# Gate rows of an xLSTM, attention and mixer kernel: laid out by kind, first two chunks built on chip, plan renewed

## The chip, the cores and the metric

One Trainium2 chip, one of its cores. The metric is device time in microseconds (us) of one launch; lower is better. Engines: PE multiplies matrices (its weight loads are PEld), DVE and ACT and POOL work on elements, SP issues transfers (its queue is SPq). "Off chip" below is the device memory that holds the inputs and the output.

## The reference

Three stages on a batch of 2 with 768 tokens. First a matrix-memory recurrence with 8 heads of 40 columns, then a two-of-four mixture of causal attention experts, then a mixer over tokens and channels.

```python
for t in range(S):                                   # 768 tokens, batch 2, 8 heads, D = 40
    m_new = np.maximum(f_gate[:, :, t] + m, i_gate[:, :, t])
    f_stab = np.exp(f_gate[:, :, t] + m - m_new)
    i_stab = np.exp(i_gate[:, :, t] - m_new)
    C = f_stab * C + i_stab * outer(vt, kt);  n = f_stab * n + i_stab * kt
    y[:, :, t] = sigmoid(o_gate[:, :, t]) * (C @ qt) / np.maximum(np.abs(n @ qt), 1.0)
# x = y with the heads side by side (320 columns)
# experts e = 0..3: softmax(causal(x wq_e (x wk_e)^T / 8)) (x wv_e) wo_e, weighted for the best 2 of 4
# u = x + (relu(x^T w_tok1) w_tok2)^T;  out = u + relu(u w_ch1) w_ch2
```

## The kernel before

**Stages.** The recurrence is cut into 6 chunks of 128 tokens per batch, so 12 chunks n = 0 to 11. For a chunk, `m_gates` makes the exponents of decay between its tokens as a product of two thin operands: `lt` (left, 128 columns) and the row tile `RT[n % 2]` (right, 4 heads x 128 tokens); ACT takes the exponential into `e`, POOL clears the part above the diagonal. `m_whole` multiplies keys and queries (both in the chunk's `kv` tile), `m_scores` multiplies that by `e` on DVE, `m_carry` and `m_decay` bring in the state `CB` of earlier chunks (through `mc` and `w`), `m_intra` sums over values and ends with x, which is transposed (`turn`) and split into a high and a low part; `m_update` makes the next state with `vs`. Two chunks of x make a stretch of 256 tokens, for which `p_qk` and `p_v` project (tiles `xt`, `wh`, `wl`); then come attention (`a_scores`, `a_unit`, `a_value`, `a_tail`), the token mixer (`t_hidden`, `t_mix`) and the channel mixer (`c_hidden`, `c_out`, 12 slices of 128 channels).

**Gates.** The decay's exponents need running sums and running maxima of the gates (`gt`), which DVE scans make: for chunk 0 in straight code (L385 to L402), for the others in `gates_rest` in pieces of one, two and two chunks. 128 partitions hold two halves of the heads and both batches, 32 each; in each 32 some rows hold a high part, some a remainder, some constants. The result `msp` stands in partitions by head and is wanted along the free axis in two partitions of the row tile, so `load_m` moves it with two transfers of 4 KB on chip (L381) per chunk. Chunk 0 alone goes another way: `lr0` and `m0` (L396 to L402), a product on DVE that spreads the heads.

**Narrowing.** The mixer's weights come as 64-bit words. `narrow` cuts each piece to 32 bits and splits it: an ACT pass (L523), three DVE passes (L526, L528, L531), for a channel piece an ACT copy (L538) and a subtraction on DVE or POOL (L292). Token weights have 8 pieces, channel weights 24.

**Order.** All instructions are put in order at build time by `Plan`: every part yields steps with an engine (or a choice), a cost, the events it waits for and the tiles it takes. The planner starts, again and again, the step that can begin first; among steps of one engine within 0.004 us the lower number in `RANK` wins. `fillers` puts products of a zero tile (`still`, 128 x 128, bf16) on PE wherever the plan has PE waiting in its first 46 us (`FILL`), which keep its clock up. The times in the plan are the planner's; on the chip only the order and the waits remain, so a filler once written is always run. SP issues transfers in the planned order, with at most 8 under way.

Of the kernel before, what the change touches and what calls it, by code (L numbers as in the profile page):

```python
# [24 lines left out]
L = 128  # L25
# [5 lines left out]
ND = 13  # L31
# [6 lines left out]
SML = 35  # L38
# [36 lines left out]
class Plan:  # L75
# [106 lines left out]
    def run(self):  # L182
        while self.live:
# [8 lines left out]
            for e, cs in cand.items():  # L192
                s0 = min(c[0] for c in cs)
                c = min((c for c in cs if c[0] <= s0 + 0.004), key=lambda c: c[1][0])
                if pick is None or c[0] < pick[1][0]:
                    pick = (e, c)
# [56 lines left out]
def fused_kernel(ctx: ExitStack, tc: tile.TileContext, gates0, gates1, kv, og, wqkv, wo, wt12,  # L253
# [50 lines left out]
    plan = Plan(dict(P=1.1, A=7.3, V=7.7, G=6.5, S=3.6),  # L304
                dict(bank=7, page=NS, rows=ROWS - 4, big=ND - 5, e=EB, w=WB, mc=1, rem=1, x=1, vs=4, xp=3, q=2,
                     am=6, atr=2, tile=2, y=2, tf=2, g=1), [0.0] * DEEP + [3.6, 2.5, 6.2, 7.8], fillers)
# [56 lines left out]
    lt = big([128, 2, S], F32R, "lt")  # L363
# [882 lines left out]
```

## Time and profile before

| | |
|---|---|
| Median of 3 runs (lowest, highest) | 357.08 us (356.17, 357.26) |
| The profiled execution | 357.03 us |
| Its span (first to last instruction) | 355.3 us |
| Busy in the span: PE, PEld | 347.2 us (98%), 303.2 us (85%) |
| Busy in the span: DVE, ACT, POOL | 233.7 us (66%), 167.4 us (47%), 37.1 us (10%) |
| Products of the zero tile | 379 of 3213 on PE |
| Bytes moved | 28.9 MB, 81 GB/s over the span |

The span is what the trace shows, the time also has what lies around it (1.73 us here). A busy share is a mean over stages with different limits: PE's 98% contains the zero products, and it is DVE that is busiest beside it until about 140 us. What ends a wait in one stage is read from that stage.

### The profile page before, as it was taken

The page shows a single profiled execution, that of the slowest core. Times are in us where ns is not written, and L with a number is a line of the kernel's source. Part 1 is how long each engine was busy: PE and PEld are TensorE (multiplying, and loading weights), DVE is VectorE, ACT ScalarE, POOL GpSimd, SP SyncE. Part 2 cuts the span into 40 slices and gives each one's busy share as a digit, 9 for nine tenths or more (in the row PEclk, how much of TensorE's full clock was granted, in tenths as well). Part 3 has the DMA queues.
Part 4 walks back from the last instruction along what each step waited for, and adds up shares of the span by engine and source line. Part 5 has one row for each costly group of instructions (what it writes and reads, how often), then busy time and mean ns, then how long its engine had stood idle before and what let it go on. Part 6 is the DMA issues. An engine that isn't in the chain of part 4 may idle for free.

```text
span 355.3 us, 7997 instructions
## 1 busy us (share of the span) xinstructions
PE 347.2 (98%) x3213; PEld 303.2 (85%) x3213; DVE 233.7 (66%) x663; ACT 167.4 (47%) x405; POOL 37.1 (10%) x64
## 2 busy tenths in 40 slices
PE   8999998999999999999999999999999999999996
PEld 8997897988889778787777788999899888998895
DVE  3799997999999989765977846996143111322122
ACT  4886655765766576565655744563221212112110
POOL 5104623231340000000000000000000000000000
PEclk9999998999999999999999999999999999999999
DMA  7993522732521132002000250400002000200002
GB/s 250 406 363 104 196 68 88 276 120 70 196 92 46 39 119 89 3 6 78 2 0 3 74 157 15 164 0 3 1 0 76 0 2 0 74 2 0 2 0 74
DMA packets 10161, 28.92 MB, mean 81 GB/s; under 512 B 1244, under 2 KB 3212, under 8 KB 10124
## 3 DMA queue, kind: packets, MB, share of 16 engines
q1 hardware_dynamic: 9980, 28.40, 22.8%
q8 instruction: 25, 0.41, 0.5%
q14 instruction: 12, 0.10, 0.1%
q10 hardware_dynamic: 144, 0.02, 0.0%
HBM read 26.35 MB, written 1.97 MB: 80 GB/s over the span
## 4 chain that ended last, share of the span: by engine, by line
PE 73%; DVE 20%; issue 2%; DMA 2%; ACT 2%; POOL 0%; DVEq 0%; POOLq 0%; SPq 0%; ACTq 0%
PE bank L268 67%; PE bank L918 4%; DVE e L635 3%; DMA raw<-in_dram 2%; DVE am L901 2%; DVE tf L531 2%; DVE tf L528 1%; PE bank L671 1%; DVE cb L748 1%; DVE x L709 1%; DVE vs L295 1%; DVE lt L375 1%; DVE w L295 1%; PE bank L943 1%; DVE cw L292 1%
## 5 line engine op out<-in xcount | busy, mean ns | idle before, releaser
L1064 DVE SCALAR_TENSOR_TENSOR h<-bank,h 128x512 fp32r<-128x512 f32 x36 | 24.8, 690 | 74.1 <-ACT h L1062 73.9
L268 PE MATMUL bank<-ut,cw 128*128 128x512 f32 x288 | 71.8, 396 | 0.0
L268 PE MATMUL bank<-cw,h 128*128 128x320 f32 x432 | 68.5, 310 | 0.0
L268 PEld LDWEIGHTS bank<-cw,h 128*128 128x128 f32 x432 | 65.3, 188 | 2.0
L1062 ACT ACTIVATE h<-bank 128x512 fp32r<-128x512 f32 x36 | 21.5, 598 | 92.1 <-PE bank L268 92.1
L268 PEld LDWEIGHTS bank<-ut,cw 128*128 128x128 f32 x288 | 52.9, 188 | 10.7 <-issue 0.2
L907 ACT ACTIVATE am<-am,mn 128x128 f32<-128x128 f32 (+5 forms) x48 | 31.8, 665 | 26.6 <-DVE mn L901 13.4
L901 DVE CUSTOM_DVE_ANT_0 am<-bank,mk 128x384 f32<-128x384 f32 (+3 forms) x64 | 30.0, 501 | 3.6 <-PE bank L268 3.4
L268 PE MATMUL bank<-still 128*128 128x128 bf16 x379 | 25.1, 232 | 1.0 <-POOL still L314 1.0
L268 PE MATMUL bank<-xt,wh 128*128 128x256 f32 x144 | 25.8, 288 | 0.1
L268 PEld LDWEIGHTS <-still 128*128 128x128 bf16 x379 | 23.8, 105 | 2.1 <-POOL still L314 1.0
L918 PE MATMUL bank<-ident,am 128*128 128x128 f32 x168 | 23.6, 275 | 0.0
L602 POOL TENSOR_SCALAR_AFFINE_SELECT e<-e 128x512 f32<-128x512 f32 x24 | 16.9, 711 | 60.5 <-ACT e L599 59.1
L268 PE MATMUL bank<-ks,q 64*128 64x384 f32 (+3 forms) x128 | 22.6, 463 | 0.5 <-DVE x L709 0.4
L918 PEld LDWEIGHTS bank<-ident,am 128*128 128x128 f32 x168 | 19.4, 141 | 3.8 <-issue 0.5
L268 PEld LDWEIGHTS bank<-xt,wh 128*128 128x128 f32 x144 | 21.2, 188 | 1.3 <-DVE mn L904 0.5
L268 PE MATMUL bank<-atr,vg 128*64 128x128 f32 x336 | 21.6, 276 | 0.0
L289 ACT COPY atr<-bank 128x384 f32<-128x384 f32 (+3 forms) x47 | 19.5, 453 | 3.9 <-PE bank L918 3.7
L268 PEld LDWEIGHTS bank<-atr,vg 128*64 128x64 f32 x336 | 18.3, 137 | 3.4 <-DVE mn L901 1.3
L523 ACT ACTIVATE tf<-raw 128x384 f32<-128x384 f32 (+1 forms) x32 | 16.7, 534 | 4.9 <-DMA raw<-in_dram 2.1
L268 PEld LDWEIGHTS bank<-ks,q 64*128 64x128 f32 x128 | 11.3, 186 | 6.9 <-issue 2.3
L528 DVE SCALAR_TENSOR_TENSOR tf<-raw,tf 128x384 uint32<-128x384 uint32 (+1 forms) x32 | 16.6, 527 | 0.2
(160 smaller groups left out, 582.1 us busy)
## 6 DMA issues: line engine op xcount, KB each, us to landing
kv<-in_dram SPq DMA_DIRECT2D x12, 836.0 KB
raw<-in_dram SPq DMA_DIRECT2D x20, 384.0 KB
raw<-in_dram SPq DMA_DIRECT2D x12, 320.0 KB
os<-in_dram SPq DMA_DIRECT2D x4, 480.0 KB
out_dram<-u SPq DMA_DIRECT2D x12, 160.0 KB
raw<-in_dram SPq DMA_DIRECT2D x3, 386.0 KB
gt<-in_dram SPq DMA_DIRECT2D x1, 640.0 KB
rt<-ms SPq DMA_DIRECT2D x22, 4.0 KB
```

The source lines that it names most:

```text
L268: PE.matmul(o, lt, r, start=first, stop=last)
L289: (A.copy if e == "A" else V.tensor_copy)(o, i)
L295: (V if e == "V" else G).tensor_mul(o, a, b)
L523: A.activation(t, w[:, :, 1].bitcast(F32), AF.Copy, scale=2.0 ** -112)
L528: V.scalar_tensor_tensor(u, w[:, :, 0], 29, u, op0=OP.logical_shift_right, op1=OP.bitwise_or)
L602: G.affine_select(e, e, [[0, 4], [1, L]], OP.is_ge, 0.0, 0, -1)
L635: V.tensor_mul(EE[n, u], PS[n][u], EE[n, u])
L901: V.tensor_tensor_reduce(a[:, b0 * 128:b1 * 128], s["p", e, ci], mks, -0.125, 3e38, OP.add, OP.min, s["mn"][:, ci, e:e + 1])
L907: A.activation(a[:, 0:w], a[:, 0:w], AF.Exp, bias=s["mn"][:, z, e:e + 1], scale=-1.0, accum_out=s["sm"][:, 0, e:e + 1])
L918: PE.transpose(pt[:, k - b0], a[:, k * 128:(k + 1) * 128], ident)
L1062: A.activation(h[0], p1, AF.Relu)
L1064: V.scalar_tensor_tensor(h[1], p1, 0.0, f32(h[0]), op0=OP.max, op1=OP.subtract)
```

## The change

- **Rows by kind.** The 128 partitions of the gate tiles are laid out anew: the upper 64 hold what goes into the left operand, the lower 64 what goes into the rows. Constants of -1 and 0 are written into `lt` and into the row tiles once (`lt_rest`, memsets on DVE for the first two chunks, on POOL for the rest), so splitting takes 64 or 32 partitions where it took 128 or 64.
- **First two chunks.** Their rows are no longer moved: `m_rows(0)` and `m_rows(1)` spread `msp` over the heads on chip, one by a DVE product, one by four ACT instructions. There are four row tiles instead of two. Chunk 0 has no code of its own any more.
- **Gates in pairs.** `gates` scans chunks in pieces of two, two and two; `m_ends` makes the rows' part in a second part. Gates for two chunks arrive first (256 KB instead of 128), the rest (512 KB) after `kv` of chunk 0, which is now loaded in two transfers.
- **Narrowing gated.** The first channel weights wait until x of chunk 9 is done, output gates of the second batch until x of chunk 3.
- **Replanned.** Some costs of steps are new, some waits are new, `RANK` is another list, and `PAT` takes the place of the constant 0.004 (with the same value).

```diff
-    plan = Plan(dict(P=1.1, A=7.3, V=7.7, G=6.5, S=3.6),
+    plan = Plan(dict(P=1.1, A=2.5, V=3.6, G=8.2, S=2.8),
...
-    SP.dma_start(gt[:, :, 0:L], gates0)
-    SP.dma_start(KV[0], kv[0, 0])
-    SP.dma_start(gt[:, :, L:], gates1)
+    SP.dma_start(gt[:, :, 0:2 * L], gates0)
+    SP.dma_start(KV[0][:, 0:8 * L], kv[0, 0][:, 0:8 * L])
+    SP.dma_start(KV[0][:, 8 * L:], kv[0, 0][:, 8 * L:])
...
-    RT = [per.tile([128, 4 * L], F32R, name=f"rt{i}", tag=f"rt{i}") for i in range(2)]
+    RT = [per.tile([128, 4 * L], F32R, name=f"rt{i}", tag=f"rt{i}") for i in range(4)]
...
+    def lt_rest(e, s):
+        for u in range(2):
+            e.memset(f32(lt[32 - 32 * u:64 - 32 * u, u, s]), 0.0)
+            e.memset(f32(lt[96 - 32 * u:128 - 32 * u, u, s]), 0.0)
+            e.memset(f32(lt[64 + 32 * u:96 + 32 * u, u, s]), -1.0)
...
+    def a_parts(e, s):
         for u in range(2):
-            r = slice(64 * u, 64 * u + 64)
-            V.scalar_tensor_tensor(lt[r, u, s], f32(ha[r, s]), lom[r], av[r, s], op0=OP.mult, op1=OP.add)
+            r = slice(32 * u, 32 * u + 32)
+            sub(e, lt[r, u, s], av[r, s], f32(ha[r, s]))
...
-    s0 = slice(0, L)
-    V.tensor_tensor_scan(fl[:, s0], rz[:, s0], fl[:, s0], 0.0, OP.mult, OP.add)
...
-    V.tensor_mul(m0, sel[r0], f32(lr0[:, 1:2]).to_broadcast([96, 4, L]))
...
-    def gates_rest():
-        for a, z in ((1, 2), (2, 4), (4, 6)):
+    def gates():
+        for a, z in ((0, 2), (2, 4), (4, 6)):
...
+    def m_ends():
+        for a, z in ((0, 2), (2, 4), (4, 6)):
+            s = slice(a * L, z * L)
+            n = (z - a) * L
+            yield on(act(n), ("mt", a))
+            A.activation(hr[dn64, s], mt[dn64, s], AF.Copy, scale=lom[dn64])
+            yield on((("W", 0.16 + n / 960.0), ("G", 0.12 + n / 435.0)))
+            sub(plan.eng, msp[dn64, s], mt[dn64, s], f32(hr[dn64, s]))
...
     def m_rows(n):
...
+        if n > 1:
+            yield on(("S", 1.3), ("msp", c), *free, *((("rti", n - 1),) if n > 2 else ()), dmas=2)
+            for u in range(2):
+                p = 64 + 32 * u
+                SP.dma_start(f32(rows_of(n)[p:p + 2]).rearrange("p (h l) -> p h l", l=L),
+                             f32(msp[p + 16 * b:p + 16 * b + 8, None, c * L:(c + 1) * L]))
...
+            return
+        yield on((pool(512), dve2(512), ("A", 0.9)), ("msp", c))
+        o, m = rt(n, dn64), f32(msp[dn64, c * L:(c + 1) * L])
+        if plan.eng == "A":
+            for h in range(4):
+                A.activation(o[:, h], m, AF.Copy, scale=smlt[dn64, 17 + 4 * b + h:18 + 4 * b + h])
+        else:
+            mul(plan.eng, o, sel(n, dn64), m[:, None, :].to_broadcast([64, 4, L]))
+        mark(("rt", n))
...
-        yield on(("S", 0.5), dmas=1)
+        yield on(("S", 0.5), *((("x", 3),) if b else ()), dmas=1)
         o = OS[b, i] = rows3("os")
...
-        yield on(("S", 0.01), *((("cwhome", k - 1),) if k else ()), *((("u0", B - 1, NCH - 1),) if own else ()), take=["big"] if own else ["home"], keep=kc if own else 0)
+        yield on(("S", 0.01), ("cwhome", k - 1) if k else ("x", 9), *((("u0", B - 1, NCH - 1),) if own else ()), take=["big"] if own else ["home"], keep=kc if own else 0)
```

What this does to the order is shown at three places.

PE at the end of the first run of zero products, where the first gates come (`rt_86` and `rt_87` are the row tiles of chunks 1 and 0, `kv_72` and `kv_73` the tiles of chunks 0 and 1). Before:

```order
L268 LDWEIGHTS still
L268 MATMUL bank<-still 128x128
L268 MATMUL bank<-m_124,lr_123 128x512 x2
L268 MATMUL bank<-kv_72 128x128 x8
L268 LDWEIGHTS still
L268 MATMUL bank<-still 128x128
```

Now:

```order
L273 LDWEIGHTS still
L273 MATMUL bank<-still 128x128
L273 MATMUL bank<-rt_86,lt 128x512 x2
L273 MATMUL bank<-rt_87,lt 128x512 x2
L273 MATMUL bank<-kv_72 128x128 x8
L273 MATMUL bank<-kv_73 128x128 x8
L273 MATMUL bank<-rt_87,mc 128x512
L273 LDWEIGHTS still
L273 MATMUL bank<-still 128x128
```

The gates of two chunks, both key-query products and a carry now stand together. Ahead of them are 137 zero products where there were 112; the runs after them are 67, 8, 2, 7 and 12 where there were 50, 195, 1, 10, 8, 1 and 2, so 233 in all where there were 379. All other products are the same in number (the two of `m_124` become two of `rt`).

SP ahead of the first moved rows (`raw` 128x772 are projection weights, `os` output gates, `wo` the experts' output weights; `raw` 128x384 and 128x320, loaded before the rows shown, are channel weights). Before:

```order
L459 DMA os<-in_dram 128x960
L490 DMA raw<-in_dram 128x772
L459 DMA os<-in_dram 128x960
L490 DMA raw<-in_dram 128x772
L459 DMA os<-in_dram 128x960
L490 DMA raw<-in_dram 128x772
L333 DMA kv_73<-in_dram 128x1672
L333 DMA kv_74<-in_dram 128x1672
L507 DMA wo<-in_dram 128x640
L381 DMA rt_87<-ms 2x4x128 x2
```

Now:

```order
L404 DMA gt<-in_dram 128x2x512
L338 DMA kv_73<-in_dram 128x1672
L513 DMA raw<-in_dram 128x772
L338 DMA kv_74<-in_dram 128x1672
L513 DMA raw<-in_dram 128x772
L484 DMA os<-in_dram 128x960
L513 DMA raw<-in_dram 128x772
L484 DMA os<-in_dram 128x960
L530 DMA wo<-in_dram 128x640
L457 DMA rt_88<-ms 2x4x128 x2
L457 DMA rt_89<-ms 2x4x128 x2
```

The first moved rows were those of chunk 1 and are now those of chunk 2 (`rt_88`); two loads of output gates and three of channel weights no longer stand ahead of them.

DVE at the gates of the second piece. Before:

```order
L416 TENSOR_SCALAR zz<-gt 128x1
L419 SCALAR_TENSOR_TENSOR mh<-zz,mh,gt 128x128
L423 SCALAR_TENSOR_TENSOR ms<-mh,smlt 128x128
L295 TENSOR_TENSOR vs<-kv_72,e 128x164
L526 TENSOR_SCALAR tf<-tf 128x384
L635 TENSOR_TENSOR e<-bank,e 128x512
L375 SCALAR_TENSOR_TENSOR lt<-ms,smlt,gt 64x128 x2
L528 SCALAR_TENSOR_TENSOR tf<-raw,tf 128x384
L478 TENSOR_TENSOR mpf<-mh,gt 128x1
L479 CAST mp<-mpf 128x1
L480 SCALAR_TENSOR_TENSOR mp<-mp,smlt,mpf 128x1
L531 SCALAR_TENSOR_TENSOR tf<-raw,minus,tf 128x384
```

Now:

```order
L414 SCALAR_TENSOR_TENSOR gt<-zz,gt 128x256
L297 TENSOR_TENSOR gt<-gt 128x256
L418 TENSOR_SCALAR zz<-gt 128x2
L300 TENSOR_TENSOR vs<-kv_72,e 128x164
L652 TENSOR_TENSOR e<-bank,e 128x512
L421 SCALAR_TENSOR_TENSOR mh<-zz,mh,gt 128x256
L297 TENSOR_TENSOR wl<-raw,wh 128x772
L300 TENSOR_TENSOR w<-w,kv_73 128x512
L297 TENSOR_TENSOR ms<-mh 64x256
L300 TENSOR_TENSOR vs<-kv_72,e 128x164
```

The narrowing passes (`tf`, `cw`) are gone from between the gates. Up to the low half of x of the second chunk, after which the first projection can go, DVE's list held 14 narrowing instructions and now holds none.

## Rows read from the trace of the kernel before

**Rows 1.** The page: span, and busy time of each engine.

```profile
span 355.3 us, 7997 instructions
...
PE 347.2 (98%) x3213; PEld 303.2 (85%) x3213; DVE 233.7 (66%) x663; ACT 167.4 (47%) x405; POOL 37.1 (10%) x64
```

**Rows 2.** Windows: length, busy us (x instructions) by engine, PE clock, DMA share, GB/s.

```profile
0.00:6.40 6.40, 5.35 (x51) 5.36 (x52) 2.80 (x10) 3.09 (x7) 4.97 (x17) 1.00 0.62 187
6.40:20.00 13.60, 13.60 (x238) 12.97 (x237) 9.12 (x27) 10.14 (x17) 1.69 (x3) 1.00 1.04 409
20.00:43.40 23.40, 22.87 (x388) 19.68 (x385) 22.79 (x54) 16.90 (x42) 8.89 (x12) 1.00 0.57 200
...
51.00:57.60 6.60, 4.99 (x54) 4.00 (x55) 6.41 (x17) 4.00 (x11) 3.77 (x4) 1.00 0.37 131
57.60:61.00 3.40, 3.40 (x55) 3.22 (x52) 2.73 (x18) 1.92 (x10) 0.00 (x0) 0.50 0.25 38
61.00:140.00 79.00, 77.62 (x939) 67.83 (x937) 74.70 (x228) 52.58 (x141) 15.10 (x25) 1.00 0.35 122
```

**Rows 3.** The same view for instructions on the zero tile alone (PE, PEld, ACT, POOL).

```profile
1.05:6.35 5.30, 5.30 (x50) 5.30 (x51) 0.20 (x1) 0.00 (x0) 1.00 0.74 223
6.35:9.90 3.55, 3.55 (x65) 3.47 (x62) 0.00 (x0) 0.00 (x0) 1.00 1.03 411
11.45:14.35 2.90, 2.90 (x50) 2.79 (x50) 0.00 (x0) 0.00 (x0) 1.00 1.01 396
15.00:25.80 10.80, 10.80 (x194) 10.80 (x195) 0.00 (x0) 0.00 (x0) 1.00 0.98 376
```

**Rows 4.** Timeline of PE, 9.9 to 43.6 us: start, us, what, count.

```profile
9.93 0.50 PE L268 MATMUL bank<-m,lr 32*128 32x512 f32 x2
10.36 1.16 PE L268 MATMUL bank<-kv 40*128 40x128 f32 x16
...
14.97 11.06 PE L268 MATMUL bank<-still 128*128 128x128 bf16 x195
25.84 0.70 PE L268 MATMUL bank<-rt,lt 128*128 128x512 f32 x2
26.64 0.49 PE L268 MATMUL bank<-rt,mc 128*128 128x512 f32 x1
...
28.32 1.13 PE L268 MATMUL bank<-kv,e 128*64 128x41 f32 x32
...
33.42 0.79 PE L268 MATMUL bank<-cb,w 128*64 128x82 f32 x16
...
43.44 0.36 PE L268 MATMUL bank<-xt,wh 128*128 128x256 f32 x1
```

**Rows 5.** Timeline of DVE and SP, first 16 us.

```profile
3.80 0.42 DVE L385 TENSOR_TENSOR_SCAN gt<-zz,gt 128x128 f32<-128x128 f32 x1 [2.48 <-DMA gt<-in_dram]
...
6.44 0.69 DVE L402 TENSOR_TENSOR m<-smlt,lr 96x512 fp32r<-96x512 f32 x1
...
15.79 1.75 SPq L381 DMA_DIRECT2D rt<-ms  x2
```

**Rows 6.** Groups by line and shape: count, busy us, mean ns, idle before.

```profile
L528 DVE SCALAR_TENSOR_TENSOR tf<-raw,tf 128x384 uint32<-128x384 uint32 x20 | 11.0, 552 | 0.1
L531 DVE SCALAR_TENSOR_TENSOR tf<-raw,minus,tf 128x384 uint32<-128x384 uint32 x16 | 9.8, 611 | 0.1
L526 DVE TENSOR_SCALAR tf<-tf 128x384 uint32<-128x384 uint32 x20 | 7.3, 368 | 1.6 <-ACT tf L523 1.6
...
L419 DVE TENSOR_TENSOR_SCAN mh<-zz,mh,gt 128x256 f32<-128x256 f32 x2 | 1.5, 750 | 0.0
```

**Rows 7.** Timeline of DVE and POOL: the same DVE product alone and beside POOL.

```profile
33.84 0.32 DVE L295 TENSOR_TENSOR vs<-kv,e 128x164 f32<-128x164 f32 x1
...
41.53 0.88 POOL L602 TENSOR_SCALAR_AFFINE_SELECT e<-e 128x512 f32<-128x512 f32 x1 [1.79 <-ACT e L599]
...
41.83 0.76 DVE L295 TENSOR_TENSOR vs<-kv,e 128x164 f32<-128x164 f32 x1
```

More of the change, by code (lines that the diff above doesn't have):

```diff
@@ L193, in run @@
                 s0 = min(c[0] for c in cs)
-                c = min((c for c in cs if c[0] <= s0 + 0.004), key=lambda c: c[1][0])
+                c = min((c for c in cs if c[0] <= s0 + PAT[e]), key=lambda c: c[1][0])
+                if c[0] > s0 + 0.004:
+                    fits = [x for x in cs if x[0] + x[2] <= c[0] + 0.03]
+                    c = min(fits, key=lambda c: c[1][0]) if fits else c
                 if pick is None or c[0] < pick[1][0]:
@@ L357, in fused_kernel @@
         G.memset(t, 0.0)
-    lt = big([128, 2, S], F32R, "lt")
+    lt_rest(G, slice(2 * L, S))
+    for i in range(2, 4):
+        G.memset(f32(RT[i][dn64]), 0.0)
     mh = big([128, 2, S], F32, "mh")
@@ L396, in fused_kernel @@
-    V.tensor_scalar(lr0[:, 1], f32(msp[r0, s0]), smlt[r0, 29:30], smlt[r0, 30:31], op0=OP.mult, op1=OP.add)
-    for u in range(2):
-        r = slice(64 * u, 64 * u + 32)
-        A.activation(lr0[r, 0], f32(lt[r, u, s0]), AF.Identity, bias=smlt[r, 32:33], scale=smlt[r, 31:32])
-    for n in range(2):
-        heads("A", n)
-    V.tensor_mul(m0, sel[r0], f32(lr0[:, 1:2]).to_broadcast([96, 4, L]))
-    mark(("rt", 0), 7.4)
-    mark(("kv", 0), 6.2)
-    mark(("gates", 0))
-    mark("gtl", 7.9)
@@ L408, in gates_rest, with gates_in @@
-    def gates_rest():
-        for a, z in ((1, 2), (2, 4), (4, 6)):
+            r = slice(32 * u, 32 * u + 32)
+            sub(e, lt[r, u, s], av[r, s], f32(ha[r, s]))
+    mark(("kq", 0), 6.6)
+    mark(("kv", 0), 7.5)
+    mark(("gtl", 0), 4.1)
+    def gates_in():
+        yield on(("S", 0.45), dmas=1)
+        SP.dma_start(gt[:, :, 2 * L:], gates1)
+        lag = plan.landed(524)
+        mark(("gtl", 2), lag)
+        mark(("gtl", 4), lag)
+    def gates():
+        for a, z in ((0, 2), (2, 4), (4, 6)):
@@ new lines, in gates @@
+            yield on((("W", 0.35 + n / 480.0), ("G", 0.3 + n / 218.0)))
+            a_parts(plan.eng, s)
+            for c in range(a, z):
+                mark(("lt", c))
+            yield on((("W", 0.55), ("G", 0.9)))
+            carry(G if plan.eng == "G" else V, a or 1, z)
+            mark(("mp", a))
+        mark("dec")
+    def m_ends():
[6 more added lines that the diff above has]
+            sub(plan.eng, msp[dn64, s], mt[dn64, s], f32(hr[dn64, s]))
+            for c in range(a, z):
+                mark(("msp", c))
+        yield on(("S", 0.0), "dec")
@@ L432, in gates_rest @@
         give("big", 3)
-        mark("dec")
     def m_rows(n):
         b, c = divmod(n, NCH)
-        free = (("mg", n - 2),) if n > 1 else ()
-        if b and c < 2:
+        free = (("mg", n - 2),) if n > 3 else ()
+        if n < 4 or c < 2:
             yield on((act(512), dve2(512)), *free)
-            heads(plan.eng, n)
-        yield on(("S", 1.3), ("gates", c), *free, *((("rti", n - 1),) if n > 1 else ()), dmas=2)
-        load_m(n)
-        mark(("rti", n))
-        plan.landed(8)
@@ L655, in m_carry @@
         give("bank")
-        dc = DEC[n] = work.tile([128, 4], F32, name="dc", tag="dc", bufs=2)
-        yield on((("A", 0.1), ("W", 0.1), ("G", 0.2)))
-        copy(plan.eng, dc, w[:, :, L - 1])
-        mark(("dec", n))
+        if c < NCH - 1:
+            old = n - 2 if c > 2 else n - 4
+            yield on((("A", 0.1), ("W", 0.1), ("G", 0.2)), *((("cd", old),) if old > 0 else ()))
+            dc = DEC[n] = work.tile([128, 4], F32, name="dc", tag="dc", bufs=2)
+            copy(plan.eng, dc, w[:, :, L - 1])
+            mark(("dec", n))
         yield on((pool(512), dve2(512)), ("kv", n))
@@ L695, in m_intra @@
         kv_used(n)
-        yield on(("A", 0.1))
-        dn = work.tile([128, 2, H], F32, name="dn", tag="dn")
+        yield on(("A", 0.1), *((("x", n - 3),) if n > 2 else ()))
+        dn = work.tile([128, 2, H], F32, name="dn", tag="dn", bufs=3)
         A.activation(dn[:, 0], t[:, :, D], AF.Abs)
-        yield on(("V", 0.32))
+        yield on(("W", 0.33))
         V.tensor_scalar(dn[:, 0], dn[:, 0], 1.0, None, op0=OP.max)
@@ L799, in p_qk @@
         else:
-            yield on((act(512), dve(512)), take=["big"] * (st == 0), keep=kl)
+            yield on((act(512), dve(512)), *((("ks", b),) if st else ()), take=["big"] * (st == 0), keep=kl)
             if st == 0:
                 KS[b] = big([128, 2, S], F32, "ks")
+                mark(("ks", b))
             copy(plan.eng, KS[b][:, :, t0:t0 + 256], pq)
@@ L812, in p_v @@
         ts_ = slice((c % 2) * 128, (c % 2) * 128 + 128)
-        yield on(pe(8, 260), *xready(b, st), *((("v", b, c - 1),) if c else ()), take=["bank"] + ["big"] * (c == 0), keep={"big": kl})
+        yield on(("P", 1.04), *xready(b, st), *((("v", b, c - 1),) if c else ()), take=["bank"] + ["big"] * (c == 0), keep={"big": kl})
         if c == 0:
@@ L827, in p_rank @@
         n = c1 - c0
-        yield on(("W", 0.5 if n > 2 else 0.3), *[("v", b, c) for c in range(c0, c1)], take=["g"])
+        yield on(("W", 0.58 if n > 2 else 0.42), *[("v", b, c) for c in range(c0, c1)], take=["g"])
         lg = VG[b][:, c0:c1, 256:260]
@@ L990, in t_hidden @@
         for c in range(NCH):
-            yield on(("P", 0.56), ("u0", b, c), ("tw", 0), take=["bank"] if c == 0 else (), keep=2 if c == 0 else 0)
+            yield on(("P", 0.535), ("u0", b, c), ("tw", 0), take=["bank"] if c == 0 else (), keep=2 if c == 0 else 0)
             if c == 0:
@@ L1098, in freed @@
         give("big", 2)
-    add(gates_rest())
+    add(gates_in())
+    add(gates())
+    add(m_ends())
     for n in range(4):
@@ L1110, in fused_kernel @@
             add(kv_in(n))
-            add(m_rows(n))
+        add(m_rows(n))
         for u in range(2):
```

155 lines of the change are left out of this document (63 added, 92 removed), and 39 rows, old and new, of the table RANK.

## The prediction

> **What bounds the kernel now.** The page comes first: PE is busy 347.2 of 355.3 us [rows 1], so a change that does not take work from PE, or end its waits, can win little. The second question is what that work is. The windows of the zero tile alone [rows 3] answer it for the first 26 us: four stretches there hold nothing else. In the last of them, 15.00 to 25.80, PE runs 194 zero products and no product of the kernel. These fillers are counted as busy, so the share of 98% hides a wait. What the wait is for stands in the timelines [rows 4, 5]: chunk 0 is through PE's first steps by 15 us, and the next product of use is the gates of chunk 1 at 25.84. The rows that it reads are moved by two transfers issued at 15.79, while the DMA engines are 0.98 busy [rows 3] with the loads ahead of them. The order on SP and the bytes bound it: with 128, 836, 640, four times 480, 384, 320, 384, three times 386, twice 836 and 320 KB ahead (sizes from the shapes in the order, 4 bytes an element), 7.95 MB had to land first; 187 GB/s for 6.4 us bring 1.2 MB and 409 GB/s after that [rows 2] the rest at 22.9 us. So in this stage the wait that ends last is the transfer, and behind it PE goes on with the fillers that the plan put there.
>
> The windows over all engines [rows 2] then show two other limits. From 20.00 to 43.40 and from 61.00 to 140.00 DVE is nearly as full as PE (22.79 of 23.40, 74.70 of 79.00). And between 51.00 and 57.60 PE works only 4.99 of 6.60 us, with DVE at 6.41: there DVE is the bound. In the 3.40 us that follow, the granted clock is 0.50: 1.2 GHz, the lower of its two levels, where the other windows have 2.4 GHz.
>
> **The change, part by part.**
>
> *Fillers, the main term.* The order has 233 zero products where it had 379, 146 fewer. At the upper clock one takes 55.7 ns (10.80 us for 194 [rows 3]). 146 x 0.0557 = **-8.1 us**. Other products are the same in number. Position by position: the first run is 137 instead of 112, so the first gates come 25 x 0.0557 = 1.4 us later, at 9.93 + 1.4 = 11.3 [rows 4]; after that 96 instead of 267 fillers, -9.5 us. The first projection, at 43.44 now [rows 4], would come at 35.3. What stands before it is otherwise nearly the same: a pair of gates, a key-query product and a carry less (0.70 + 1.16 + 0.49 [rows 4]), a state product and an intra product more (0.79 + 1.13), made good later. I take 0 for that.
>
> A filler gone helps only if what PE then reaches is ready. Three covers have to hold.
>
> *Cover 1, gates of the first pair.* Twice the gates arrive: 128 KB more at 187 GB/s [rows 2] put the first scan at 3.80 + 0.7 = 4.5 us [rows 5]. Then two scans of 256 columns (0.75 each, the dearer of the two [rows 6]), and five more DVE or ACT instructions in a row that the trace does not have in this form (64 or 32 partitions, 256 or 512 columns). The nearest is the product of 96 x 512 at 0.69 [rows 5]; none has more columns, so 5 x 0.69 bounds them from above, and nothing bounds them from below. Ready by 4.5 + 1.5 + 3.45 = 9.5 us at the latest; four ACT instructions for chunk 0's rows run beside DVE's and would have to take over 0.45 each more to matter. PE reaches the gates at 11.3, so this is covered by 1.8 us: cost 0. Before it was the same: the rows were ready at 7.13 (6.44 + 0.69) and PE came at 9.93 [rows 4, 5], since the first 50 fillers run at 106 ns each, half the later pace [rows 3].
>
> *Cover 2, rows of chunk 2.* They are the first that are still moved. Ahead of them 256, 836, 512, twice 836, three times 386, twice 480 and 320 KB stand on SP, 5.85 MB: 1.2 MB by 6.4 us and the rest at 409 GB/s, landed at 17.8. PE wants them after 11.3 + two pairs of gates, two key-query products and a carry (4.2 us), 67 fillers (3.7), and two `vs` products, two intra products and a state product (4.6, `vs` taken as the state product's 0.79): 23.8 us. Covered by 6 us. If the 3 us that lie between 22.9 and 25.84 above are all issue and landing, still by 3.
>
> *Cover 3, DVE up to the first projection.* From the scan of the second pair to the low half of x of chunk 1 DVE now has 40 instructions; in 20.00 to 43.40 it did 54 in 22.79, 0.42 each [rows 2]. The first of them that needs the new chunk's exponents can start at about 13 us (11.3 + gates 0.35, exponential and select). Had none of the 40 been done by then, 13 + 40 x 0.42 = 29.8. PE is there at 35.3. So DVE is ahead by some 5 us, where before it was the bound: its list held 14 narrowing passes before that point (0.37, 0.55 and 0.61 us for the kinds in [rows 6]), and they now wait for x of chunk 9.
>
> *DVE from 40 to 61 us.* If DVE is ahead there too, the 1.61 us that PE idles in 51.00 to 57.60 and what the clock takes from 57.60 to 61.00 (at half rate 3.40 us do what 1.70 would) can go: bounds 0 and -3.3. I take **-2.0**, nearer to the gain, as PE comes 8 us earlier but 14 passes at about 0.5 us have left DVE's list. The passes are not lost: they come back between chunk 9 and the end, where DVE is less full. In 61.00 to 140.00 PE idles 1.38 us in all; with DVE's list fuller there, I leave that as it is.
>
> *POOL.* It gets element work in the fill stage (`lt` parts, small sums, more memsets). One DVE product took 0.32 alone and 0.76 while POOL ran a select [rows 7]; so each DVE instruction beside a new POOL one may cost up to 0.44. There are two of 256 columns and three small ones between 13 and 24 us, so 0 to 2.2 us of DVE, inside cover 3. On PE's path I take **+0.3**, bounds 0 and 1.
>
> The page "GPSIMD Engine Reference" of the Trainium skill (Key points) says that POOL shares its SBUF interfaces with VectorE and disturbs DVE instructions with two SBUF inputs. The two rows agree with it. By that rule alone every one of the five would cost DVE in full, and the sum would be 2.2 instead of 0.3 on this line.
>
> *Later waits and queues.* Loads of the second batch's output gates wait for x of chunk 3, and SP is in order, so what is queued behind them waits too: in the order those are two token weight pieces and rows of later chunks, wanted tens of us later. Cost 0; if the cover fails, a late row costs PE a filler-free wait, counted in the second rival.
>
> **Sum.** -8.1 - 2.0 + 0.3 = -9.8 us. The profiled execution took 357.03 us (span 355.3), 0.05 under the median of the runs, so no correction: **347.2 us**.
>
> **Rivals.**
>
> *DVE takes over.* The fillers go, but PE then stands idle for DVE in 20 to 60 us, as it does at 51.00 to 57.60 now. For it: DVE is already full there [rows 2]. Against it: cover 3. Price: half to all of the 5 us of cover turned into waits, and none of the 2.0 gained: 350 to 355 us.
>
> *DVE is relieved for good.* All 3.3 us of the stretch go, and the 1.38 us in 61.00 to 140.00 too: 357.03 - 8.1 - 4.7 = 344.3, say 342.5 to 345.
>
> *The transfers still end the wait.* If the rows of chunk 2 come as late as those of chunk 1 did (25.84), or 8 us later in the queue's second half, the change does not do what it says: PE waits at 23.8 for as long as the fillers saved, 356 to 358 us.
>
> *The clock falls, slower than before.* The fillers keep PE's clock up, and the trace shows what happens without: after the thin stretch at 51.00 the clock is 0.50 for 3.40 us. With 146 fewer fillers the stretch from 18 to 35 us is thin as well, and products there would run at half rate. Price: the 17 us of this stretch at half rate are 17 more, 347.2 + 17 = 364. It decides against the change once more than 8 us of work at the upper clock run at the lower. Against it: from 28 to 43 us PE now has only some 20 fillers, and the granted clock of 20.00 to 43.40 is 1.00 [rows 2].
>
> The page "TensorE: Matmul & The Clock Gate" of the Trainium skill (Part 1) states that the array is throttled by default and that activity releases it, and that idling brings half rate back. The 106 ns pace of the first 50 fillers and the 0.50 after 57.60 agree [rows 2, 3]. By that rule fewer fillers are a risk in themselves, which is this rival.
>
> **How the numbers follow.** Forecast (345 to 350) 0.52; DVE takes over (350 to 355) 0.22; relieved for good (under 345) 0.17; transfers still end it 0.04; the clock 0.05. The range reaches from 343.4 to 352.3: it holds the forecast, most of the third case and about half of the first rival, about 0.8 in all. A run of this kernel can tell 0.3% (1.1 us) from no change. Faster by more than that: 0.52 + 0.22 + 0.17 = 0.91; within it 0.04, the transfers; slower 0.05, the clock.
>
> **What would show it.** Right: zero products in four or five runs that add up to 233; gates of two chunks at about 11.3 us; gates of chunk 2 with no idle time before them at about 24; the first projection at 33 to 36; the granted clock at 1.00 in the stretch up to 60 us; DVE with no `tf` instruction before 45 us. Wrong: idle time on PE before 60 us that DVE ends (the first rival), a wait of PE at the first moved rows that a transfer ends (the third), or windows before 60 us with the clock at 0.50 (the last). A first projection at 35 with a time above 352 would mean that the gain is given back after 60 us, for which I have no mechanism.

## The result and the profile after

| | before | after |
|---|---|---|
| Median (lowest, highest), same chip | 356.62 us (355.56, 357.26) | 343.92 us (343.43, 344.98) |
| The profiled execution, its span | 357.03, 355.3 us | 344.98, 343.3 us |
| Products of the zero tile | 379 | 233 |
| First projection on PE starts at | 43.44 us | 35.41 us |
| From there to the end of the span | 311.9 us | 307.9 us |

The ratio of the medians is 0.9651, with a 95% interval from 0.9616 to 0.9686. The change is faster by 12.7 us where 9.8 were forecast; 343.92 lies inside the range, at its lower end. The last two rows divide the 12.0 us of the span: 8.0 are won before the first projection and 4.0 behind it.

The start of a trace is to be read with care. The first zero products run at half pace [rows 3], and the half pace does not end at a fixed time: the same 137 products took 10.59 us in after (first row) and 9.11 in the run a_nofill (second row; the run is described below), because it lasted until 6.9 us in the one and 3.8 in the other. Over all the traces here the end lies between 3.7 and 7.0 us, so two executions can differ by some 1.5 us at their start without any difference in the kernel. Where that matters, times are counted from the first gates.

```profile
1.05 10.59 PE L273 MATMUL bank<-still 128*128 128x128 bf16 x137 [1.05 <-POOL still L319]
...
1.05 9.11 PE L273 MATMUL bank<-still 128*128 128x128 bf16 x137 [1.05 <-POOL still L319]
```

The page of after has the same 98% for PE as [rows 1], with 10.7 us less work.

```profile
span 343.3 us, 7706 instructions
...
PE 336.5 (98%) x3067; PEld 293.4 (85%) x3067; DVE 231.1 (67%) x653; ACT 167.4 (49%) x405; POOL 45.6 (13%) x80
```

The timeline of PE answers to [rows 4]. The gates of two chunks come in one piece at 11.45, behind them one run of zero products is left that lasts longer than a microsecond, and the gates of chunk 2, the first that need moved rows, start at 22.90 with no idle time ahead of them. Between the first gates and the first projection the only wait that a named engine ends is the one at 32.12.

```profile
11.45 1.17 PE L273 MATMUL bank<-rt,lt 128*128 128x512 f32 x4
...
14.88 3.92 PE L273 MATMUL bank<-still 128*128 128x128 bf16 x67
...
22.90 0.73 PE L273 MATMUL bank<-rt,lt 128*128 128x512 f32 x2
...
32.12 0.79 PE L273 MATMUL bank<-cb,w 128*64 128x82 f32 x16 [0.79 <-DVE w L300]
...
35.41 0.39 PE L273 MATMUL bank<-xt,wh 128*128 128x256 f32 x1
```

The windows (columns as in [rows 2]) show the other 4 us. The first two rows reach from the first projection to the end, before and after: PE idles 4.42 us instead of 6.51 and is busy for 1.88 less. The other rows, all of after, show where. From 51.00 to 57.60 PE is busy all the time where it idled for 1.61; from 57.60 to 61.00 the granted clock is 1.00 where it was 0.50, worth 1.70; from 61.00 to 140.00 PE idles 0.65 instead of 1.38. Against that, from 43.40 to 51.00 it idles 0.39 where it idled 0.07. Together that is 3.7 of the 4.0. These windows are rougher than the first two rows, since PE is 8 us further in its work after the change. The fall of the clock is no accident of one profile: the mean granted clock was 0.990 to 0.995 in every execution of before on record, and 0.998 to 1.000 in every one of after.

```profile
43.44:355.30 311.86, 305.35 (x2544) 265.20 (x2543) 198.99 (x577) 137.22 (x342) 21.54 (x33) 0.99 0.17 56
...
35.41:343.30 307.89, 303.47 (x2517) 263.59 (x2513) 201.40 (x585) 146.54 (x362) 26.15 (x39) 1.00 0.21 69
...
20.00:43.40 23.40, 22.42 (x353) 19.69 (x350) 22.39 (x59) 12.43 (x33) 6.07 (x11) 1.00 0.44 154
43.40:51.00 7.60, 7.21 (x58) 6.80 (x57) 5.98 (x25) 6.47 (x18) 1.92 (x3) 1.00 0.66 222
51.00:57.60 6.60, 6.60 (x123) 5.74 (x122) 5.72 (x25) 6.38 (x19) 3.42 (x7) 1.00 0.13 23
57.60:61.00 3.40, 3.40 (x34) 2.53 (x34) 3.37 (x9) 2.40 (x8) 1.59 (x3) 1.00 0.53 218
61.00:140.00 79.00, 78.35 (x946) 66.96 (x943) 76.09 (x228) 53.50 (x135) 15.36 (x21) 1.00 0.39 130
```

Six more rows of after belong to the covers. The product that makes chunk 0's rows ends at 8.86, 2.6 us before PE comes. DVE has chunk 2's rows ready (`ms`) at 18.31, and SP issues them at 18.39. DVE's `w` takes 1.62 us where POOL's `w` of another chunk runs beside it; PE's wait at 32.12 ends with it. And the low half of x of chunk 1 (`xt`) is done at 33.25.

```profile
8.17 0.69 DVE L300 TENSOR_TENSOR rt<-smlt,ms 64x512 fp32r<-64x512 f32 x1
...
17.47 0.84 DVE L297 TENSOR_TENSOR ms<-mh 64x256 fp32r<-64x256 f32 x1
...
18.39 2.87 SPq L457 DMA_DIRECT2D rt<-ms  x4
...
30.25 1.27 POOL L300 TENSOR_TENSOR w<-w,kv 128x512 f32<-128x512 f32 x1
...
30.45 1.62 DVE L300 TENSOR_TENSOR w<-w,kv 128x512 f32<-128x512 f32 x1
...
32.70 0.55 DVE L742 TENSOR_TENSOR xt<-bank,xt 128x384 fp32r<-128x384 f32 x1
```

### The profile page after: what moved, and what is told of

Its sections match the earlier page's. It is cut to its first block, busy times and chain, and to the rows that moved or that the text cites. A ratio compares the mean times of both kernels' runs of the same rounds, so it can differ in the third digit from the quotient of the medians.

```text
span 343.3 us, 7706 instructions
## 1 busy us (share of the span) xinstructions
PE 336.5 (98%) x3067; PEld 293.4 (85%) x3067; DVE 231.1 (67%) x653; ACT 167.4 (49%) x405; POOL 45.6 (13%) x80
## 4 chain that ended last, share of the span: by engine, by line
PE 86%; DVE 5%; ACT 4%; DMA 2%; issue 1%; SPq 1%; POOL 0%; DVEq 0%; ACTq 0%; POOLq 0%
PE bank L273 79%; PE bank L938 4%; DMA os<-in_dram 2%; PE bank L690 1%; DVE e L652 1%; ACT am L927 1%; ACT atr L294 1%; PE bank L963 1%; SPq L457 1%; PE bank L691 1%; ACT os L487 1%; ACT os L490 1%; DVE am L921 1%; DVE u L1106 1%; DVE w L300 0%
## 5 line engine op out<-in xcount | busy, mean ns | idle before, releaser
L273 PE MATMUL bank<-still 128*128 128x128 bf16 x233 | 16.8, 241 | 1.1 <-POOL still L319 1.1
L273 PEld LDWEIGHTS <-still 128*128 128x128 bf16 x233 | 15.9, 110 | 1.6 <-POOL still L319 1.0
L554 DVE SCALAR_TENSOR_TENSOR tf<-raw,minus,tf 128x384 uint32<-128x384 uint32 (+1 forms) x28 | 16.5, 593 | 0.2
```

The source lines that it names most:

```text
L273: PE.matmul(o, lt, r, start=first, stop=last)
L554: V.scalar_tensor_tensor((hi if lo is None else t).bitcast(U32), w[:, :, 1], minus.bitcast(U32), u, op0=OP.bitwise_and, op1=OP.bitwise_or)
```

## The experiments

Two theories stood against each other. **Theory:** the change gains in two separate places; zero products go because the rows of chunk 1 no longer wait for a transfer (8 us), and DVE's list before 61 us gets shorter because the narrowing has left it (4 us). **Rival:** the second gain, or both, come from the renewed order as a whole. A planner makes it hard to tell these apart, since a changed wait gives another order everywhere. So in the first four runs only the zero products differ and all else keeps its order. In the other six the order of before or after was written down step by step and replayed, with only the named steps moved. The replayed kernels have other line numbers, since the list of steps stands in the file. Ratios are to the kernel before on the same chip, whose median was 356.2, 356.3 and 356.2 us in the three batches. After itself was not run again in them (356.6 for before where it ran), so a difference to after, or from one batch to another, is uncertain by about half a microsecond.

### What a zero product costs: a_more, a_trim, b_trim

**a_more**: after, with 45 zero products more in the first run.

```diff
-            self.fill(n)
+            self.fill(n + 45 if self.first else n)
+            self.first = False
```

> The changed kernel with 45 zero products more in the first run (182 for 137), nothing else moved. Theory A: 45 x 0.0557 = 2.5 us longer, 346.4. Rival (DVE sets the pace, PE has slack): the 0.8 us for which PE waits for DVE at 32 us is used up first, so 1.7 us or less longer, 345.6 or under.

Measured: 347.19 us, ratio 0.9746 [0.9713, 0.9778]. That is 3.3 us more than after for 45 x 0.0557 = 2.5 us of products. The traces settle it: from the first gates to the end of the span it is 345.5 - 13.48 = 332.0 us here and 343.3 - 11.45 = 331.9 in after. So zero products on this path cost their own time, and nothing behind them makes it good.

```profile
13.48 1.17 PE L274 MATMUL bank<-rt,lt 128*128 128x512 f32 x4
```

**a_trim**: after, with the planner told the pace that [rows 3] show for the first 50 zero products (106 ns), so that it writes 91 in the first run instead of 137.

```diff
-            self.free["P"] += self.stream(self.free["P"], 0.056, 0.95)
+            self.free["P"] += self.stream(self.free["P"], 0.107 if self.free["P"] < 6.4 else 0.056, 0.95)
```

> The changed kernel with 46 zero products fewer in the first run (91 for 137); every other instruction in the same order. In its trace the rows of chunks 0 and 1 are ready at 8.86 us, and PE comes to the gates at 11.45, since the first 50 zero products take 106 ns each, not the 56 that the plan reckons with. Theory A (PE's list sets the end, the chain behind the gates has slack): gates at 9.0 to 9.2, the whole kernel 2.3 us shorter, 341.6. Rival (loads or DVE set the pace of the fill stage): idle time in place of the zero products, 343.5 to 344.

Measured: 342.04 us, ratio 0.9606 [0.9578, 0.9634]. The timeline of PE shows where cover 1 ends: the gates now wait for DVE's `rt` by 1.24 us and start at 9.01, and the first projection comes 2.3 us earlier than in after.

```profile
9.01 1.17 PE L273 MATMUL bank<-rt,lt 128*128 128x512 f32 x4 [1.24 <-DVE rt L300]
...
29.83 0.79 PE L273 MATMUL bank<-cb,w 128*64 128x82 f32 x16 [0.80 <-DVE w L300]
...
33.12 0.39 PE L273 MATMUL bank<-xt,wh 128*128 128x256 f32 x1
```

**b_trim**: the same edit in before, 66 instead of 112 in the first run.

> The kernel before with 46 zero products fewer in the first run (66 for 112), nothing else moved. If the moved rows of chunk 1 bound its start (my account: landed at 23 us or later, asked for at 25.84): PE comes to them at 23.3, waits for up to some 2 us, and the kernel is 0.5 to 2.5 us shorter, 354.1 to 356.1, with idle time ended by the transfer. Rival (the rows had long landed, the zero products alone held PE): all of 2.5 us, 354.1, and no idle time there.

Measured: 355.02 us, ratio 0.9961 [0.9930, 0.9993]. The gates of chunk 1 start 2.35 us earlier than at 25.84 [rows 4]. So in before the transfer was not quite what ended the wait: the rows' last DMA packet is at 22.6 us here and at 23.0 in before, and for some 2 us behind them the zero products ran on. The planner believed in a later time than the chip's.

Little of it stays, for two reasons. Right behind these gates 1.54 us are lost to ACT, and then the granted clock falls to 0.52 from 26.00 to 33.00, so that the first projection comes at 44.61, later than in before. The ten executions show what the clock takes: the two with a mean clock of 0.999 and 1.000 took 352.8 us, the eight with 0.995 or less 354.4 to 356.6.

```profile
23.49 0.70 PE L268 MATMUL bank<-rt,lt 128*128 128x512 f32 x2 [0.30 <-DVE gt L413]
25.74 0.49 PE L268 MATMUL bank<-rt,mc 128*128 128x512 f32 x1 [1.54 <-ACT mc L644]
...
44.61 0.36 PE L268 MATMUL bank<-xt,wh 128*128 128x256 f32 x1
```

```profile
26.00:33.00 7.00, 7.00 (x65) 5.60 (x64) 6.76 (x19) 5.08 (x15) 2.40 (x4) 0.52 0.32 97
```

### What the zero products are for: a_nofill

After without any zero product behind the first run (96 fewer).

```diff
-        while self.free["P"] + 0.17 < s:
+        while self.free["P"] + 0.17 < s and self.free["P"] < 8.75:
```

> The changed kernel without the 96 zero products behind the first run (5.3 us of PE), nothing else moved. If they only stand where PE would wait anyway and the clock does not care: 0 to 1.5 us shorter, 342.4 to 344. Rival, the clock: with PE idle from 14.9 to 19 us the granted clock falls to half in one or more stretches before 40 us; each 3.4 us at 0.50 costs up to 1.7 us, so 345 to 349.

Measured: 346.40 us, ratio 0.9728 [0.9683, 0.9773], 2.5 us slower than after, though PE has less to do. The wait that 67 zero products had filled is now an idle time of 4.13 us:

```profile
17.69 1.43 PE L273 MATMUL bank<-vs,kv 128*40 128x41 f32 x29 [4.13 <-issue]
```

The windows show the granted clock at 0.74 from 15 to 20 us and at 0.61 and 0.71 from 30 to 40, where after has 1.00; the mean clock was 0.984 to 0.988 in all four executions.

```profile
15.00:20.00 5.00, 2.31 (x52) 2.35 (x53) 4.89 (x10) 4.04 (x5) 2.86 (x6) 0.74 0.60 238
...
30.00:35.00 5.00, 3.92 (x72) 3.81 (x70) 4.23 (x7) 0.18 (x1) 0.86 (x1) 0.61 0.00 0
35.00:40.00 5.00, 5.00 (x62) 4.92 (x59) 3.33 (x11) 0.46 (x2) 0.00 (x0) 0.71 0.29 74
```

So the rival with the clock describes a real mechanism; after keeps enough zero products that it doesn't happen.

### The narrowing alone: b_late, b_late_cut, a_early

**b_late**: the order of before, replayed, with all 379 zero products; six channel pieces leave the first 62 us. On SP:

```diff
-DMA os<-in_dram 128x960
-DMA raw<-in_dram 128x384
-DMA raw<-in_dram 128x320
-DMA raw<-in_dram 128x384
-DMA os<-in_dram 128x960
+DMA os<-in_dram 128x960 x2
...
-DMA raw<-in_dram 128x320 x2
...
-DMA raw<-in_dram 128x384
```

> The order of before, kept step by step with the same 379 zero products; only the loads and passes that narrow the first three channel blocks (six pieces, 24 passes of DVE or POOL and 12 of ACT) are taken out of the first 62 us and put between 130 and 195 us. Theory (DVE's list was the bound between 40 and 61 us): PE reaches the first projection at 43.4 as before, the 1.61 us of idle time in 51.00 to 57.60 and the clock at 0.50 in 57.60 to 61.00 go, and the time falls by 3.3 to 4.7 us, to 351.5 to 353 beside 356.2. Rival (the gain of the change behind the first projection comes from the other order, not from the passes): within 1 us of before, 355 to 356.5.

Measured: 353.45 us, ratio 0.9917 [0.9888, 0.9947], 2.9 us gained, a little less than the theory's 3.3 to 4.7. The windows from 51.00 to 61.00 look like those of after: no idle time to speak of, and the clock at 1.00.

```profile
51.00:57.60 6.60, 6.55 (x128) 5.74 (x128) 6.15 (x29) 6.11 (x24) 3.44 (x5) 1.00 0.49 164
57.60:61.00 3.40, 3.40 (x47) 3.19 (x44) 3.26 (x15) 2.34 (x10) 1.49 (x3) 1.00 1.00 401
```

In the timeline of PE the first projection comes at 41.98, 1.5 us earlier than before, which had not been expected. Of that, 0.9 lies ahead of the first gates (9.01 instead of 9.93 [rows 4], with the same 112 zero products ahead of them): the half pace ended earlier in this execution, and that is not the narrowing's doing. A new wait of 1.15 us at 153.21 gives some of it back, where the moved passes now stand on DVE's list. From the first projection to the end it is 311.9 - (351.4 - 41.98) = 2.4 us less; without the new wait it would be 3.6, of the 4.0 that after shows.

```profile
9.01 0.50 PE L333 MATMUL bank<-m,lr 32*128 32x512 f32 x2
...
41.98 0.36 PE L333 MATMUL bank<-xt,wh 128*128 128x256 f32 x1
...
153.21 0.44 PE L1008 MATMUL bank<-ident,c 128*128 128x128 f32 x2 [1.15 <-DVE c L360]
```

So most of the second gain is the narrowing's, its passes and loads together, with no change of the order around it. For this gain the rival falls.

**b_late_cut**: the same, with 95 zero products instead of 195 ahead of the gates of chunk 1.

> The same with 95 zero products instead of 195 in the run ahead of the gates of chunk 1. Theory (the rows of chunk 1 were late because of the bytes ahead of them on SP, and 1.41 MB of those, 3.4 us at 409 GB/s, were these channel pieces): the rows land at 19.5 instead of 22.9, PE comes to the gates at 20.3 and hardly waits, and 4 to 5.6 us are gained on top of the run with 195. Rival (it takes rows made on chip): the gates still come at 22.9 or later, with idle time ahead of them, and at most 3 us are gained.

Measured: 350.71 us, ratio 0.9844 [0.9808, 0.9880], 2.7 us gained on top. Neither side was quite right: that is within the rival's 3 us, but the gates come at 20.86, earlier than its 22.9. The theory's 19.5 rested on a slip. 1.41 MB are four channel pieces, and only three had stood ahead of these rows: 1.11 MB, or 2.7 us, which gives 20.2. In the trace the rows' last DMA packet is at 20.0, and PE starts 0.8 us after it.

```profile
20.86 0.70 PE L333 MATMUL bank<-rt,lt 128*128 128x512 f32 x2 [1.65 <-DMA rt<-ms]
...
38.77 0.36 PE L333 MATMUL bank<-xt,wh 128*128 128x256 f32 x1
```

Moving the narrowing is thus worth 356.3 - 350.7 = 5.6 us in all, without a new layout of the rows, once 100 zero products go with it; the remaining 7 us or so of the change need the rest of it. What the later loads of output gates, the new costs of steps and the new `RANK` contribute by themselves, no run separates.

**a_early**: the reverse, the order of after with five channel pieces from 20 us on. The beginning of it on DVE:

```diff
 TENSOR_TENSOR cb<-cb,bank 40x4x41 x2
+TENSOR_SCALAR tf<-tf 128x384
 TENSOR_TENSOR wh<-raw,wh 64x772
+SCALAR_TENSOR_TENSOR tf<-raw,tf 128x384
 TENSOR_TENSOR x<-os,dn 128x320
+SCALAR_TENSOR_TENSOR tf<-raw,minus,tf 128x384
 TENSOR_SCALAR dn<-dn 128x8
```

> The order of after, kept step by step with the same 233 zero products; five pieces of channel weights (20 passes of DVE or POOL, 10 of ACT) are loaded and narrowed from 20 us on, one pass after each third step, instead of behind x of chunk 9. Theory (the cover of DVE is some 5 us, and the passes take 9 to 10): PE waits for DVE by 4 to 6 us before 61 us, nothing is given back later, 348 to 350. Rival (DVE has room there): within 1 us of after, 343 to 345.

Measured: 353.58 us, ratio 0.9910 [0.9874, 0.9946], 9.7 us slower than after and more than expected. PE waits for DVE several times, and the clock falls behind the waits:

```profile
27.88 0.48 PE L752 MATMUL bank<-ident,x 128*128 128x128 f32 x2 [2.02 <-DVE x L790]
...
36.79 0.79 PE L335 MATMUL bank<-cb,w 128*64 128x82 f32 x16 [1.36 <-DVE w L362]
...
42.12 0.39 PE L335 MATMUL bank<-xt,wh 128*128 128x256 f32 x1
```

```profile
20.00:43.40 23.40, 17.94 (x259) 14.94 (x260) 21.08 (x49) 10.67 (x26) 7.06 (x10) 0.85 0.44 153
51.00:57.60 6.60, 6.60 (x43) 6.23 (x43) 5.04 (x27) 4.92 (x17) 0.77 (x4) 0.74 0.73 263
```

The first projection is 6.7 us later than in after. Without the gate on the narrowing, the first rival (DVE takes over) would have come true in this order.

### The rows made on chip: a_rows1

The order of after, replayed; chunk 1's rows go by transfer again.

```diff
-        if n > 1:
+        if n > 0:
             yield on(("S", 1.3), ("msp", c), *free, *((("rti", n - 1),) if n > 2 else ()), dmas=2)
```

> The order of after, kept step by step with the same 233 zero products; only chunk 1's exponent rows are moved by two transfers again, issued on SP behind the third load of gate weights, where after makes them on chip with four ACT instructions. Theory (rows made on chip are what lets the gates of two chunks go at once): 4.9 MB stand ahead of the rows on SP, they land at 15 to 16 us, PE comes to the gates of chunk 1 at 12.0 and waits 3 to 4 us, which nothing behind makes good: 347 to 348. Rival (the wait falls into the 67 zero products that follow, or the rows land in time): 344 to 345.

Measured: 351.98 us, ratio 0.9888 [0.9864, 0.9913], 8.1 us slower than after. PE waits 6.08 us for the transfer, nearly twice what was expected, in part because it was there 0.9 us sooner than reckoned; the rows' last DMA packet is at 16.2, and PE starts 1.0 us after it. The first projection is back at 43.50:

```profile
17.23 1.19 PE L335 MATMUL bank<-rt,lt 128*128 128x512 f32 x2 [6.08 <-DMA rt<-ms]
22.66 5.15 PE L335 MATMUL bank<-still 128*128 128x128 bf16 x67
...
43.50 0.39 PE L335 MATMUL bank<-xt,wh 128*128 128x256 f32 x1
```

The windows explain the other 2 us: with PE empty from 12.00 to 17.00, the clock is 0.50 in the 5 us that follow.

```profile
12.00:17.00 5.00, 0.00 (x0) 0.00 (x0) 0.33 (x1) 0.00 (x0) 0.32 (x1) 0.80 1.02 410
17.00:22.00 5.00, 4.77 (x34) 3.99 (x34) 1.52 (x3) 2.30 (x4) 2.24 (x4) 0.50 0.19 75
```

Making these rows on chip is worth 8.1 us in this order. A planner that knew of the transfer would put other work there, so this is the price of this part with all else held, and another order may pay less; no run shows that.

### Towards a faster one: a_trim_w, a_best

**a_trim_w**: a_trim, replayed, with `w` of chunk 2 on DVE instead of POOL.

> The order of after with 46 zero products fewer in the first run (342.0 alone), and one product more moved from POOL to DVE: the w of chunk 2, which now runs on POOL for 1.27 us while DVE's own w of chunk 3 takes 1.62 instead of 0.69. Theory (the two hold each other up): the two on DVE one behind the other take 1.4 us, the idle time of 0.8 ahead of the first product on cb and w falls to 0.3 or less, and the time is 341.2 to 341.7. Rival (DVE's list is what is short there, so any product more on it costs): idle time of 1 us or more, 342 to 343.

Measured: 341.14 us, ratio 0.9578 [0.9553, 0.9604], the best of all runs, though its executions overlap with those of a_trim. The traces, whose first gates both start at 9.01, show the gain more surely. The two products take 0.69 and 0.68 on DVE, where the one beside POOL's had taken 1.62; the idle time at `cb,w` is gone and the first projection comes at 32.17 instead of 33.12.

```profile
28.13 0.69 DVE L362 TENSOR_TENSOR w<-w,kv 128x512 f32<-128x512 f32 x1
29.46 0.68 DVE L362 TENSOR_TENSOR w<-w,kv 128x512 f32<-128x512 f32 x1
...
32.17 0.39 PE L335 MATMUL bank<-xt,wh 128*128 128x256 f32 x1
```

One on each engine took 1.82 us in after, from the first start to the last end; on DVE alone the two need 0.69 + 0.68 = 1.37. The page "GPSIMD Engine Reference" of the Trainium skill (Specifications) states that POOL shares its SBUF interfaces with VectorE, with contention for DVE instructions with two SBUF inputs; by that rule DVE's product is held up, and the trace agrees, with 1.62 us beside 0.69.

**a_best**: a_trim_w with the products on `vs` further up on DVE's list, one of them taken over from POOL. With it go 43 zero products, and on ACT a pass on a gate weight (`wh`) moves behind the first output gates. On DVE:

```diff
-TENSOR_TENSOR wl<-raw,wh 128x772
-TENSOR_TENSOR w<-w,kv 128x512
-TENSOR_TENSOR ms<-mh 64x256
 TENSOR_TENSOR vs<-kv,e 128x164
 TENSOR_TENSOR vs<-kv,e 128x164
+TENSOR_TENSOR vs<-kv,e 128x164
+TENSOR_TENSOR ms<-mh 64x256
```

> The order with 46 zero products fewer and w of chunk 2 on DVE (341.1), with DVE's list from 13 to 20 us in another order: the four products that scale v ahead of w of chunk 1, of the low half of a gate weight and of the moved rows, the fourth of them on DVE instead of POOL, and 24 zero products instead of 67 behind the first carry. Theory (PE's 3.9 us of zero products there stand for a place far back on DVE's list): the products on vs start at some 14.5 instead of 16.9, the gates of chunk 2 at 18.3 instead of 20.6, and 1 to 2.4 us are gained: 338.8 to 340.2. Rival (what is brought forward is missing later, DVE being full from 20 to 43 us): the idle time comes back ahead of the products on cb and w near 28 us, 340.8 to 342.

Measured: 345.27 us, ratio 0.9692 [0.9664, 0.9720], 4.1 us slower than a_trim_w. The first half went as expected: `vs` at 13.98, gates of chunk 2 at 19.07, and the transfer ends a short wait there.

```profile
13.98 1.04 PE L335 MATMUL bank<-vs,kv 128*40 128x41 f32 x32
...
19.07 0.70 PE L335 MATMUL bank<-rt,lt 128*128 128x512 f32 x2 [0.16 <-DMA rt<-ms]
...
23.90 0.50 PE L335 MATMUL bank<-rt,mc 128*128 128x512 f32 x1 [2.48 <-ACT mc L723]
...
36.08 0.38 PE L335 MATMUL bank<-xt,wh 128*128 128x256 f32 x1
```

Then PE waits 2.48 us for ACT, neither of the two things expected. ACT works in order, and on its list the first output gates had to wait for their load; from 17.24 on it is busy up to the end of the `mc` that PE waits for:

```profile
17.24 1.01 ACT L549 ACTIVATE os<-os 128x960 f32<-128x960 f32 x1 [2.74 <-DMA os<-in_dram]
```

```profile
20.00:43.40 23.40, 20.65 (x261) 17.82 (x258) 20.48 (x55) 12.14 (x30) 4.14 (x8) 0.85 0.37 135
```

The clock falls to 0.85 on average from 20.00 to 43.40, and all is lost. It takes about half of that: the one execution at a mean clock of 1.000 took 343.4 us, still 2.3 more than a_trim_w. So the 3.9 us of zero products in after seem to stand not only for DVE's list but also for ACT's and for this load; no run changes the load and ACT's order one at a time.

## Why the prediction was right, and what was mis-sized

- **What bounds.** Right: in the first 26 us it was the place of the rows of chunk 1 on SP (a_rows1, b_late_cut), then DVE's list (b_late, a_early). One correction: the last 2 us ahead of 25.84 were not the transfer's but zero products too many (b_trim).
- **Fillers, -8.1.** Right: 233 are left, the gates came at 11.45 (11.3 forecast), the first projection at 35.41 (35.3 forecast), so 8.0 were gained. a_more shows that such products cost their own time.
- **Cover 1.** Held: rows ready at 8.86 (9.5 at the latest), PE 2.6 us later. a_trim used this cover up.
- **Cover 2.** Held, but the step behind it was wrong. The forecast took the bytes ahead on SP for what bounds these rows, landed at 17.8; that fits a_best, where their last packet is at 18.1. In after it is DVE's list: the rows are ready at 18.31 and issued at 18.39, their last packet is at 20.6, and with the 0.8 to 1.0 us from there to PE's start (b_late_cut, a_rows1) some 1.3 us are left until PE comes at 22.90, not 6.
- **Cover 3.** Held by less than forecast. The low half of x of chunk 1 is done at 33.25, not at 29.8, so DVE is 2.2 us ahead of PE at the first projection and not 5: from 13.37 on its 38 instructions took 0.52 us each, not 0.42. At `w` it is behind already, by the wait of 0.79. a_trim does not use this cover up, since DVE's list moves along with PE there (the wait stays at 0.80). The passes that a_early puts there cost 9.7 us, as much as the 9 to 10 that they were reckoned at, part of it by the clock.
- **DVE from 40 to 61 us, -2.0.** This is the term that was mis-sized. 4.0 were measured from the first projection to the end: the whole bound of 3.3 went, and of the 1.38 us from 61.00 to 140.00, which the prediction left as they were, another 0.73, less 0.3 of new idle time from 43.40 to 51.00. The reason given for stopping short, PE coming 8 us earlier, was outweighed by the passes that had left. b_late shows that the narrowing alone does most of it. This is the rival "DVE is relieved for good", which had 0.17; its 344.3 is within 0.4 of the result, though not all of the 1.38 went.
- **POOL, +0.3.** The size was near: from 20.00 to 43.40 PE idles 0.98 instead of 0.53. The place was not foreseen; it is one wait behind two `w`, which a_trim_w takes away, and not the small sums.
- **The clock.** The rival did not come, since the granted clock is 1.00 throughout; but b_trim (46 zero products fewer in before), a_nofill (96 fewer in after) and a_rows1 show its mechanism at work. The page "TensorE: Matmul & The Clock Gate" of the Trainium skill (Part 1) says that idling brings half rate back; by that rule a_rows1's empty 5 us must cost more than themselves, and the trace agrees, with 0.50 in the next 5 us.
- **The sum.** The forecast had -7.8 ahead of the first projection (the fillers and POOL's 0.3) and -2.0 behind it; -8.0 and -4.0 were measured, all of the 12.05 between the two profiled executions (357.03 and 344.98). After's median lies a further 1.1 under its own profiled execution, whose half pace at the start was nearly the longest of all traces. With that the result stands 0.5 inside the lower end of the range, so the range held with little to spare.

## What to carry to other kernels

Filler work counts as busy, so take the share of PE apart by tile before believing it, and give the planner a pace that traces show: a wrong pace for the first 50 fillers alone cost some 1.9 us in after. One trace is not enough for it, since the half pace ended anywhere from 3.7 to 7.0 us. With 91 fillers instead of 137 the first gates started at 9.01 in all three traces (a_trim, a_trim_w, a_best), whether it ended at 4.2 or at 7.0: PE waits there for DVE's rows, or comes just in time. Fewer are not always better: where the clock falls, it takes back what they gave (b_trim, a_nofill). Work that is not due for a long time is not free because its engine seems to have room; moved behind the stage where that engine's list is what the next one waits for, it won 2.9 us with nothing else changed, and 5.6 with the fillers cut that had stood for its bytes in the queue. A cover belongs to the instruction that is waited for, so when one engine's list is rearranged, look at which load or which other engine's list had stood hidden behind it.

## What the runs showed of the hardware

- The same DVE product of 128 x 512 took 0.69 us alone, and 1.62 beside the same product on POOL, which took 1.27: one after the other on DVE the two need 1.37.
- The half pace of the first zero products, from 1.05 us on, ended between 3.7 us (b_late_cut) and 7.0 us (a_trim_w) with the same instructions on PE up to there; after had 6.9, a_nofill 3.8.
- An empty stretch of 5 us on PE was followed by 5 us at a granted clock of 0.50, 1.2 GHz, although PE was busy for 4.77 of them; the first run of zero products, at half pace until 6.35 [rows 3], has 1.00 in the same column, so there the pace tells more than the column.
- Rows moved by transfers of 4 KB behind a filled queue had their last packet where the bytes ahead put it, at 409 GB/s: 16.2 us where these give 15.8 (5.03 MB, a_rows1), 20.0 where they give 20.2 (6.83 MB, b_late_cut). PE started 1.0 and 0.8 us after that packet, and 1.0 in a_best.
